# Turning attention weights on VectorE and through DRAM instead of on TensorE, with the order of every engine written out

## The chip, the cores and the metric

One core of one Trainium2 chip runs the kernel. The metric is device time in microseconds (us), the median of the runs on the chip; a profiled execution gives the traces that are quoted.

## The reference

```python
# q, k, v: (8, 8, 576, 64) fp32: batch, heads, sequence, head dimension
scores = q @ k.T / 8
thresh = max(scores, -1) - tau                        # tau = 0.02
scores = where(scores >= thresh, scores, -1e9)
attn = exp(scores - max(scores)); attn /= attn.sum(-1) + 1e-9
x = (attn @ v)  -> (4608, 512)                        # heads side by side
h = x @ w_in                                          # 512 -> 2048
g = where(h > 0, h, exp(min(h, 0)) - 1)
return g @ w_out                                      # 2048 -> 512
```

## The kernel before

Work goes in steps of 128 query rows (the 64 left over rows of two heads share a step, a half step) of a pair of heads: five steps a pair, 20 a sequence, 160 in all. A step computes scores, their maximum, the exponentials, masks them (`w`), normalises, and turns the 128 x 1152 weights on TensorE, so that keys lie on the partitions for the product with `v`. A whole sequence's result then goes through the feed-forward part in 32 units of four 512-column matmuls (in the profile a matmul of fp32 shows as two records). From step 20 the units are mixed in between the attention steps, so that TensorE has work during the waits of attention. The weights w_in and w_out arrive as 64-bit floats and are converted on the way, in the first 35 steps.

```python
    # ... (pools, constants, weight conversion, loads of q, k, v are cut)
    def begin(pr, i, hs):
        qT, kT, qd = pairs[pr][:3]
        if hs[0] == 0:
            open_steps[pr, i] = {
                "w": att.tile([P, 2, 2, HALF], FP32, name="w"),
                **{x: small.tile([P, 2], FP32, name=x) for x in ("mx", "nb", "th", "sm", "rs")},
            }
        st = open_steps[pr, i]
        cs = slice(hs[0], hs[-1] + 1)
        scs = {h: psum["s"].tile([P, 2, 512], FP32, name="sc") for h in hs}
        for a in range(2):
            for h in hs:
                k0 = a * HALF + (0 if h else TAIL)
                r, qs = (slice(h * D, (h + 1) * D), qT[:, i * P : (i + 1) * P]) if i < NC else (slice(0, P), qd)
                nc.tensor.matmul(scs[h][:, a, :HALF], qs[r], kT[r, k0 : k0 + HALF], start=True, stop=True)
        for h in hs:
            nc.vector.tensor_reduce(st["mx"][:, h : h + 1], scs[h][:, :, :HALF], axis=AX.XY, op=ALU.max)
        nc.gpsimd.tensor_scalar(st["nb"][:, cs], st["mx"][:, cs], nkeep, 1.0, ALU.mult, ALU.mult)
        nc.gpsimd.tensor_scalar(st["th"][:, cs], st["mx"][:, cs], 1.0, ntau, ALU.mult, ALU.add)
        for h in hs:
            e = att.tile([P, 2, HALF], FP32, name="e", bufs=3)
            nc.scalar.activation(e, scs[h][:, :, :HALF], AF.Exp, bias=st["nb"][:, h : h + 1], scale=keep)
            st[h] = scs[h], e

    def finish(pr, i, hs):
        st = open_steps[pr, i]
        cs = slice(hs[0], hs[-1] + 1)
        w, sm, rs = st["w"], st["sm"], st["rs"]
        for h in hs:
            sc, e = st.pop(h)
            nc.vector.scalar_tensor_tensor(w[:, h], sc[:, :, :HALF], st["th"][:, h : h + 1], e, ALU.is_ge, ALU.mult,
                                           accum_out=sm[:, h : h + 1])
        nc.vector.tensor_scalar(sm[:, cs], sm[:, cs], 1e-9, None, ALU.add)
        nc.vector.reciprocal(rs[:, cs], sm[:, cs])
        for h in hs:
            nc.gpsimd.tensor_scalar(w[:, h], w[:, h], rs[:, h : h + 1], 1.0, ALU.mult, ALU.mult)

    def transpose(dst, src):
        nc.tensor.matmul(dst, src, ident, is_transpose=True, skip_group_check=True)

    def turn(pr, i):
        w = open_steps.pop((pr, i))["w"].rearrange("p h a n -> p (h a n)")
        if i == 0:
            wTs[pr, 0] = wtp.tile([P, 2 * NC + 1, 2 * P], FP32, name="wTa")
        if i == 2:
            wTs[pr, 1] = wtp.tile([P, 2 * NC + 1, 2 * P + TAIL], FP32, name="wTb")
        wT = wTs[pr, min(i // 2, 1)]
        n0 = i % 2 * P if i < NC else 2 * P
        if i < NC:
            cs = slice(n0, n0 + P)
            for h in range(2):
                rt = ps_t.tile([P, NC, P], FP32, name="rt", tag="rt")
                for c in range(NC):
                    k0 = h * (S + TAIL) + c * P
                    transpose(rt[:, c], w[:, k0 : k0 + P])
                nc.scalar.copy(wT[:, h * NC : (h + 1) * NC, cs], rt)
            rt = ps_t.tile([P, NC, P], FP32, name="rt", tag="rt")
            transpose(rt[:, 0], w[:, MAIN : MAIN + P])
            nc.scalar.copy(wT[:, 2 * NC, cs], rt[:, 0])
        else:
            # ... (second part of the odd tile of 64 + 64 query rows is cut)

    def values(pr, part):
        b, j = divmod(pr, NPAIR)
        vm, vd = pairs[pr][3:]
        wT = wTs.pop((pr, part))
        if b not in xts:
            xts[b] = xpool.tile([P, KJ, MAIN], FP32, name="xt")
        n = wT.shape[2]
        pv = ps_t.tile([P, 512], FP32, name="pv", tag="rt")
        nc.tensor.matmul(pv[:, :n], vd, wT[:, 2 * NC], start=True, stop=False, skip_group_check=True)
        for c in range(NC):
            for h in range(2):
                nc.tensor.matmul(pv[h * D : (h + 1) * D, :n], vm[:, h, c], wT[:, h * NC + c],
                                 start=False, stop=(c == NC - 1), skip_group_check=True)
        nc.scalar.copy(xts[b][:, j, part * 2 * P : (part + 1) * 2 * P], pv[:, : 2 * P])
        if part:
            # ... (tail columns are cut)

    def ffn1(g, ft):
        while progress[1] < (ft // 4 + 1) * KJ:
            convert_w()
        xt = xts[g] if g < B else xtail
        ph = psum["f"].tile([P, 512], FP32, name="ph", tag="f")
        for j in range(KJ):
            nc.tensor.matmul(ph, w_in_sb[:, j, ft * P : (ft + 1) * P], xt[:, j], start=(j == 0), stop=(j == KJ - 1))
        e = epool.tile([P, MAIN], FP32, name="fe")
        nc.scalar.activation(e, ph, AF.Exp)
        nc.vector.tensor_scalar(e, e, 1.0, -1.0, ALU.min, ALU.add)
        gt = gts[ft] = gpool.tile([P, MAIN], FP32, name="gt")
        nc.vector.scalar_tensor_tensor(gt, ph, 0.0, e, ALU.max, ALU.add)

    # ... (first sequence, heads one by one, is cut); then, steps 20 to 161:
    due = 0.0
    rate = (NFT + NIT * NFT // 4) / (per_seq - 1)
    for n in range(per_seq, len(steps) + 2):
        if n < len(steps):
            ahead(*steps[n])
            begin(*steps[n], [0, 1] if steps[n][1] < NC else [0])
            convert_w()
            convert_w()
            finish(*steps[n], [0, 1] if steps[n][1] < NC else [0])
        if n - 1 < len(steps):
            turn(*steps[n - 1])
        behind(*steps[n - 2])
        due = min(due + rate, len(units))
        while due >= 1 and units:
            f, a = units.popleft()
            f(*a)
            due -= 1
```

The scheduler of the language orders the instructions of each engine.

## Time and profile before

| | before |
|---|---|
| median of the runs | 1615.66 us (three runs; 1614.61 with the fourth, used below) |
| span of the profiled run | 1611.8 us |
| TensorE busy | 97% |
| VectorE, ScalarE, GpSimd busy | 46%, 36%, 24% |
| a sequence of 20 steps, once steady | 178.6 us |

How to read the groups: source line, engine, operation, output <- inputs, shapes, number; then busy time in us and mean ns of one; then the idle time of that engine just ahead of them and what ended it. In a timeline the columns are start and length in us, engine, line, operation, tiles and number, and in brackets the idle time before. Matmuls overlap their neighbours, so what one costs is the distance to the next start.

### The profile page before, as it was taken

To read this page: it belongs to the slowest core of one execution; us is meant where nothing else is said; L and a number is where in the kernel's file an instruction comes from. 1 tells how busy PE (TensorE), PEld (TensorE's weight loads), DVE (VectorE), ACT (ScalarE), POOL (GpSimd) and SP (SyncE) were. 2 spreads that over 40 slices of the span, in tenths; PEclk is the share of its full clock that TensorE was granted. 3 is DMA by queue.
4 is the path that set the end of the run, shared out by engine and by line. 5 is a ranking of instruction groups with operands and counts; after the bars stand their busy time and mean duration, and the time that the engine had idled before them with its cause. 6 is when DMAs were issued, how large, how long until landed. Compare 5 with 4: busy or idle time off the path is not lost.

```text
span 1611.8 us, 17586 instructions
## 1 busy us (share of the span) xinstructions
PE 1570.4 (97%) x5952; PEld 786.4 (49%) x5952; DVE 735.0 (46%) x1670; ACT 586.1 (36%) x1109; POOL 379.6 (24%) x779
## 2 busy tenths in 40 slices
PE   7899889999999999999999999999999999999998
PEld 4554444554454445544555544554555454444443
DVE  6778773455335543455335543455345533220210
ACT  4665653343334433344334433344234333110110
POOL 4654552221222212222122212212122222000000
PEclk8999999999999999999999999999999999999999
DMA  5334541111111101110111011111110000000000
GB/s 108 69 81 104 142 130 36 32 19 23 29 29 29 23 15 36 36 23 15 30 35 30 15 25 27 34 23 23 28 34 10 9 7 14 7 1 20 7 7 20
DMA packets 200553, 55.68 MB, mean 35 GB/s; under 512 B 191760, under 2 KB 191760, under 8 KB 200464
## 3 DMA queue, kind: packets, MB, share of 16 engines
q1 hardware_dynamic: 200464, 54.56, 15.2%
q8 instruction: 48, 0.79, 0.2%
q14 instruction: 41, 0.34, 0.1%
HBM read 45.09 MB, written 9.44 MB: 34 GB/s over the span
## 4 chain that ended last, share of the span: by engine, by line
PE 82%; DVE 7%; POOL 4%; ACT 2%; issue 2%; DMA 1%; SPq 1%; POOLq 0%; DVEq 0%; ACTq 0%
PE po L299 30%; PE ph L285 26%; PE sc L197 9%; PE rt L221 8%; PE pv L269 8%; DVE w L213 3%; POOL w L218 2%; PE pv L266 2%; DVE mx L199 1%; ACT e L204 1%; POOL wtop L134 1%; DMA wst<-in_moe_w_out_dram 1%; DVE gt L290 1%; ACT fe L287 1%; DVE fe L288 1%
## 5 line engine op out<-in xcount | busy, mean ns | idle before, releaser
L299 PE MATMUL po<-w_out_sb,gt 128*128 128x512 f32 x1152 | 520.0, 597 | 0.0
L285 PE MATMUL ph<-xt,w_in_sb 128*128 128x512 f32 x1024 | 464.1, 597 | 0.0
L199 DVE TENSOR_REDUCE mx<-sc 128x1 f32<-128x576 f32 x288 | 207.4, 751 | 304.7 <-PE sc L197 304.6
L299 PEld LDWEIGHTS po<-w_out_sb,gt 128*128 128x128 f32 x1152 | 209.7, 191 | 236.5 <-issue 236.0
L218 POOL TENSOR_SCALAR w<-w,rs 128x576 f32<-128x576 f32 x288 | 217.0, 763 | 357.3 <-DVE rs L216 326.8
L213 DVE SCALAR_TENSOR_TENSOR w<-sc,th,e 128x576 f32<-128x576 f32 x288 | 226.5, 815 | 158.5 <-ACT e L204 150.8
L285 PEld LDWEIGHTS ph<-xt,w_in_sb 128*128 128x128 f32 x1024 | 184.7, 190 | 204.0 <-issue 203.0
L204 ACT ACTIVATE e<-sc,nb,keep 128x576 f32<-128x576 f32 x288 | 227.4, 829 | 83.8 <-POOL nb L200 83.5
L221 PE MATMUL rt<-ident,w 128*128 128x128 f32 (+1 forms) x1344 | 211.5, 284 | 17.9 <-POOL w L218 12.0
L221 PEld LDWEIGHTS rt<-ident,w 128*128 128x128 f32 (+1 forms) x1344 | 153.4, 143 | 118.5 <-issue 46.1
L197 PE MATMUL sc<-kT,qT 64*128 64x288 f32 x1024 | 192.9, 439 | 16.6 <-DVE kT L172 8.2
L288 DVE TENSOR_SCALAR fe<-fe 128x512 f32<-128x512 f32 x144 | 63.7, 443 | 315.3 <-ACT fe L287 315.3
L287 ACT ACTIVATE fe<-ph 128x512 f32<-128x512 f32 x144 | 85.9, 596 | 287.8 <-PE ph L285 287.8
L197 PEld LDWEIGHTS sc<-kT,qT 64*128 64x128 f32 x1024 | 107.1, 190 | 127.1 <-issue 84.9
L200 POOL TENSOR_SCALAR nb<-mx,nkeep 128x2 f32<-128x2 f32 (+1 forms) x176 | 52.1, 296 | 480.8 <-DVE mx L199 404.9
L238 ACT COPY wTa<-rt 128x512 f32<-128x512 f32 x128 | 70.9, 587 | 163.1 <-PE rt L221 161.1
L238 ACT COPY wTb<-rt 128x512 f32<-128x512 f32 x128 | 72.2, 584 | 129.3 <-PE rt L221 128.1
L290 DVE SCALAR_TENSOR_TENSOR gt<-ph,fe 128x512 f32<-128x512 f32 x144 | 99.4, 690 | 5.8
L304 ACT COPY ot<-po 128x512 f32<-128x512 f32 x36 | 21.1, 585 | 181.4 <-PE po L299 181.4
L269 PE MATMUL pv<-wTb,vm 128*64 128x320 f32 x512 | 76.0, 439 | 0.0
L269 PE MATMUL pv<-wTa,vm 128*64 128x256 f32 x512 | 63.6, 391 | 0.0
L285 PE MATMUL ph<-xtail,w_in_sb 128*128 128x512 f32 x128 | 55.1, 592 | 0.0
(45 smaller groups left out, 666.7 us busy)
## 6 DMA issues: line engine op xcount, KB each, us to landing
qm<-in_q_dram SPq DMA_DIRECT2D x128, 72.0 KB, 2.6
km<-in_k_dram SPq DMA_DIRECT2D x128, 72.0 KB, 2.5
vm<-in_v_dram SPq DMA_DIRECT2D x64, 128.0 KB, 2.4
wst<-in_moe_w_in_dram SPq DMA_DIRECT2D x16, 512.0 KB, 4.0
wst<-in_moe_w_out_dram SPq DMA_DIRECT2D x16, 512.0 KB, 3.8
out_dram<-ot SPq DMA_DIRECT2D x32, 256.0 KB, 2.0
vd<-in_v_dram SPq DMA_DIRECT2D x64, 16.0 KB, 2.1
out_dram<-ot SPq DMA_DIRECT2D x8, 128.0 KB, 2.3
```

Of the source, the lines that this page charges most:

```text
L197: nc.tensor.matmul(scs[h][:, a, :HALF], qs[r], kT[r, k0 : k0 + HALF], start=True, stop=True)
L199: nc.vector.tensor_reduce(st["mx"][:, h : h + 1], scs[h][:, :, :HALF], axis=AX.XY, op=ALU.max)
L204: nc.scalar.activation(e, scs[h][:, :, :HALF], AF.Exp, bias=st["nb"][:, h : h + 1], scale=keep)
L213: nc.vector.scalar_tensor_tensor(w[:, h], sc[:, :, :HALF], st["th"][:, h : h + 1], e, ALU.is_ge, ALU.mult, accum_out=sm[:, h : h + 1])
L218: nc.gpsimd.tensor_scalar(w[:, h], w[:, h], rs[:, h : h + 1], 1.0, ALU.mult, ALU.mult)
L221: nc.tensor.matmul(dst, src, ident, is_transpose=True, skip_group_check=True)
L238: nc.scalar.copy(wT[:, h * NC : (h + 1) * NC, cs], rt)
L269: nc.tensor.matmul(pv[h * D : (h + 1) * D, :n], vm[:, h, c], wT[:, h * NC + c], start=False, stop=(c == NC - 1), skip_group_check=True)
L285: nc.tensor.matmul(ph, w_in_sb[:, j, ft * P : (ft + 1) * P], xt[:, j], start=(j == 0), stop=(j == KJ - 1))
L287: nc.scalar.activation(e, ph, AF.Exp)
L290: nc.vector.scalar_tensor_tensor(gt, ph, 0.0, e, ALU.max, ALU.add)
L299: nc.tensor.matmul(po[:, :DM], gts[ft][:, it * P : (it + 1) * P], w_out_sb[:, ft], start=(ft == 0), stop=(ft == NFT - 1))
```

## The change

Its intent is to take the transposes off TensorE, the engine that sets the end. From step 35 on VectorE turns the weights in 32x32 squares (`x`), four transfers write the squares to DRAM (`there`) in the order in which the turned tile needs them, and one transfer of the step after reads them back. In place of the scheduler's order stands a written one: step n computes scores, step n-1 turns, step n-2 reads back, step n-3 multiplies with `v`. Two more edits come with it and act from step 20 on: both heads share one score tile with one maximum, and the minimum-and-add of the feed-forward (`fe`) moves from VectorE to GpSimd. The turned tile also gets a new layout from the start, 32 columns to a group, and the conversion of the weights writes into its input's buffer in place of one of its own.

```diff
-            nc.vector.tensor_reduce(st["mx"][:, h : h + 1], scs[h][:, :, :HALF], axis=AX.XY, op=ALU.max)
+        nc.vector.tensor_reduce(st["mx"][:, cs], src[:, :, :, :HALF], axis=AX.XY, op=ALU.max)   # both heads
...
+    def turn_squares(pr, i):
+        w = open_steps.pop((pr, i))["w"]
+        x = late["x"].tile([P, NT, NCH, T], FP32, name="x")
+        def turn_part(c0, src, nc_):
+            nc.vector.transpose(x[:, :, c0 : c0 + nc_], src.rearrange("p (c g n) -> p g c n", c=nc_, n=T))
+        if i < NC:
+            turn_part(0, w[:, :MAIN], NC)
+            turn_part(NC, w[:, MAIN : MAIN + P], 1)
+            turn_part(NC + 1, w[:, MAIN + P :], NC)
...
+        there = turns[pr, i] = dram.tile([NT, T, NT, NCH * T], FP32, name="there")
+        for p in range(NT):
+            nc.sync.dma_start(
+                there[:, :, p].rearrange("c k n -> k c n"), x[p * T : (p + 1) * T].rearrange("k c j n -> k c (j n)")
+            )
...
-        nc.scalar.activation(e, ph, AF.Exp)
-        nc.vector.tensor_scalar(e, e, 1.0, -1.0, ALU.min, ALU.add)
-        nc.vector.scalar_tensor_tensor(gt, ph, 0.0, e, ALU.max, ALU.add)
+        return (
+            lambda: nc.scalar.activation(e, ph, AF.Exp),
+            lambda: nc.gpsimd.tensor_scalar(e, e, 1.0, -1.0, ALU.min, ALU.add),
+            lambda: nc.vector.scalar_tensor_tensor(gt, ph, 0.0, e, ALU.max, ALU.add),
+        )
...
-    for name, bufs in (("s", 2), ("f", 2)):
+    for name, bufs in (("s", 1), ("f", 2)):      # "s" is now one tile of four banks
...
+    with tc.manual_schedule():
+        posts = ()
+        for n in range(SWITCH, len(steps) + 3):  # SWITCH is 35
+            step = (*steps[n], heads_of(steps[n][1])) if n < len(steps) else None
+            due = min(due + rate, len(units))
+            if step:
+                scores(*step)
+            for post in posts[:2]:
+                post()
+            if step:
+                exponentials(*step)
+            for post in posts[2:]:
+                post()
+            if SWITCH < n <= len(steps):
+                turn_squares(*steps[n - 1])
+            if SWITCH + 1 < n <= len(steps) + 1:
+                fetch(*steps[n - 2])
+            posts = ()
+            if due >= 1:
+                posts = ffn_unit()
+                due -= 1
+            if step:
+                masks(*step)
+                # ... q or k of the next pair is prepared here
+            for post in posts:
+                post()
+            posts = ()
+            if step:
+                normalize(*step)
+            if n - 3 >= SWITCH:
+                behind(*steps[n - 3])
+            # ... loads of the pair after the next
+            if due >= 1:
+                posts = ffn_unit()
+                due -= 1
```

## The prediction

> **What bounds the kernel now.** I read the page's engine totals and slices first, then the busy time by stretch, then the groups, and last the timeline of two steps. A step is one 128-row block of queries of one pair of heads; a pair has four full steps and one half step, a sequence four pairs (20 steps), the kernel 160 steps.
>
> ```profile
> PE 1570.4 (97%) x5952; PEld 786.4 (49%) x5952; DVE 735.0 (46%) x1670; ACT 586.1 (36%) x1109; POOL 379.6 (24%) x779
> PE   7899889999999999999999999999999999999998
> DVE  6778773455335543455335543455345533220210
> DMA  5334541111111101110111011111110000000000
> ```
>
> TensorE is full from slice 7 (about 250 us) to the end; VectorE is half idle there and the DMA engines nearly idle. Busy time by stretch says it sharper (columns: stretch, length, then PE, PEld, DVE, ACT, POOL, granted clock, DMA share, GB/s):
>
> ```profile
> 210.00:220.00 10.00, 6.98 (x22) 3.96 (x22) 9.07 (x20) 5.74 (x11) 4.55 (x6) 0.84 0.53 136
> 300.00:400.00 100.00, 99.75 (x400) 50.89 (x399) 51.45 (x115) 39.23 (x75) 21.74 (x50) 1.00 0.13 24
> 600.00:700.00 100.00, 99.92 (x407) 50.46 (x406) 42.72 (x101) 35.58 (x70) 23.20 (x50) 1.00 0.15 32
> ```
>
> So there are three stages: to about 250 us VectorE and its chain decide; to 1387 us (the last value matmul) TensorE does, at 99.8%; then it runs the feed-forward part alone. By the order of instructions the change begins at step 35 (pair 7) of 160. In the timeline the maxima of pair 7 start at 265.8 us, and from then a sequence takes 178.6 us (pairs 12, 16, 20, 24, 28 at 493.7, 672.3, 850.9, 1029.5, 1208.0). The groups concerned:
>
> ```profile
> L221 PE MATMUL rt<-ident,w 128*128 128x128 f32 (+1 forms) x1344 | 211.5, 284 | 17.9 <-POOL w L218 12.0
> L199 DVE TENSOR_REDUCE mx<-sc 128x1 f32<-128x576 f32 x288 | 207.4, 751 | 304.7 <-PE sc L197 304.6
> L213 DVE SCALAR_TENSOR_TENSOR w<-sc,th,e 128x576 f32<-128x576 f32 x288 | 226.5, 815 | 158.5 <-ACT e L204 150.8
> L172 DVE STREAM_TRANSPOSE kT<-km 128x576 f32<-128x576 f32 x32 | 24.6, 769 | 1.1 <-DMA km<-in_k_dram 1.1
> L288 DVE TENSOR_SCALAR fe<-fe 128x512 f32<-128x512 f32 x144 | 63.7, 443 | 315.3 <-ACT fe L287 315.3
> ```
>
> The 211.5 us of transposes look like the prize, but a mean of 284 ns overlaps its neighbours. The timeline of TensorE gives the distance from start to start:
>
> ```profile
> 604.59 1.24 PE L197 MATMUL sc<-kT,qT 64*128 64x288 f32 x8
> 605.76 1.09 PE L221 MATMUL rt<-ident,w 128*128 128x128 f32 x8
> 606.69 1.02 PE L299 MATMUL po<-w_out_sb,gt 128*128 128x512 f32 x2
> 607.55 0.27 PE L221 MATMUL rt<-ident,w 128*128 128x128 f32 x1
> 607.66 0.62 PE L266 MATMUL pv<-wTa,vd 128*128 128x256 f32 x2
> 608.21 1.95 PE L269 MATMUL pv<-wTa,vm 128*64 128x256 f32 x16
> 610.09 2.84 PE L299 MATMUL po<-w_out_sb,gt 128*128 128x512 f32 x6
> ```
>
> Eight transposes take 0.93 us, the ninth 0.11: some 0.116 us each. In the same way: scores 1.17 us (half step 0.97), the value matmuls of the first part 2.43, of the second 2.96, one feed-forward unit (8 records of about 0.43) 3.45.
>
> **What the Trainium skill says.** "TensorE: Matmul & The Clock Gate", Part 4, gives about 275 ns for a transpose in a kernel; the trace agrees on the duration (284), yet what one costs here is the 116 ns pitch. "VectorE: DVE Perf Modes", The three transpose paths: VectorE turns 32x32 blocks only, which is why DRAM must put the squares in place. The trace has the operation at 769 ns for 576 columns. The clock page's Part 1 says an idle window of about 3.4 us halves the TensorE clock: the trace agrees in its first stage (0.84 at 210 us, TensorE 70% busy) and grants 1.00 later; so gaps under 2 us should be harmless. "SBUF — State Buffer", Who interferes with whom: a VectorE instruction with at most one SBUF input outside the two-port modes does not block GpSimd. The squares are such; the removed L288, at 443 ns for 512 elements, runs faster than one element a cycle and may well have been in such a mode. No run shows the lock.
>
> **The change, part by part** (steps 35 to 159: 125 steps, 6.25 sequences).
> 1. Removed: 42 transposes a pair, 168 a sequence, at 0.116 = 19.5 us a sequence; ACT's copies of them (about 1.44 us a step) go too, beside the path. Added on TensorE: one value matmul of 384 in place of 320 columns, 0.2 us a sequence. TensorE's own work becomes 178.6 - 19.3 = 159.3 us a sequence: 122 us over 6.25 sequences is the most there is.
> 2. Added on VectorE: the pitch in this trace is columns / 0.96 plus about 110 ns (mask and sum: 608.68 to 609.42). A full step's squares, 512 + 128 + 512 columns, are then 0.64 + 0.24 + 0.64 = 1.53 us; both heads' maximum in one instruction is 1.31 instead of 1.42. VectorE a step: 1.31 + 1.53 + masks 1.57 + sums 0.37 + up to two gelu-like combinations (gt) at 0.64 + 0.3 for q and k = 6.4 at most, against 8.0 of TensorE: not the bound on average.
> 3. The new ring. The score tile is one buffer of four banks for both heads, so scores of step n+1 wait for the second mask of step n, and in VectorE's written order the previous step's squares stand before that mask. From start of scores: 1.27 (to the maximum) + 1.31 + 1.53 + 1.57 + 0.12 (semaphore) = 5.8 us, 6.4 with a gt between. The exponentials are beside it (maximum + 1.4 us). A step with two feed-forward units keeps TensorE at work for 1.17 + 6.9 = 8.0: no wait. A step with one unit and no value matmuls offers 4.6 and stops for 1.2 (1.8 with gt). I counted the written order: in each 20 steps five are like that (four at 1.2, one at 1.8), **6.6 us a sequence**; two at the start of the new order have no unit at all, and 7 us are lost once.
> 4. q and k preparation now stands ahead of GpSimd's part of the feed-forward: a gt comes about 0.3 us late for its PSUM buffer once a sequence, 0.3 us.
> 5. DRAM. A step writes 576 KB in four transfers and reads them back in one. The trace has 512 KB landing in 4.0 us and 0.36 us to issue one such store. The read issued in step m-1 comes after its squares (4.1 to 4.7) and four issues (1.5), lands 4.4 us later, or 6.5 if it queues behind the writes: 10 to 13 us after step m-1 began. Step m needs it after scores and one unit: at 8.0 + 4.6 = 12.6 after a full step, but at 5.8 + 4.6 = 10.4 after a one-unit step, which precede five of eight value groups. I choose 3 us a sequence (possible: 0 to 10).
> 6. Steps 0 to 34 keep the TensorE transposes; there copies with more pieces and the joint score tile cost, GpSimd's taking L288 gains: I set 0, within 8 us either way.
>
> Sum: 159.3 + 6.6 + 0.3 + 3 = 169.2 us a sequence, 9.4 less than before, times 6.25 = 59 us; less 7 at the start = 52. The base of 178.6 exceeds its own terms (111 units, 22.6 scores, 21.6 values, 19.5 transposes = 175) by 3.5 us of small gaps, some of which the transposes cause, so I take a gain of 60: **1555 us**.
>
> **Rivals.** (a) Everything hides: TensorE stays at 99.8% and the whole 122 us come: about 1495. For it: VectorE's idle half; against it: the ring in 3, whose terms are all measured ones. (b) VectorE becomes the bound: if the strided squares cost twice the plain transpose, the ring is 8.0 and every step is tight: some 12 us a sequence more, about 1610 to 1630. For it: no row has this access pattern; against it: the blocks are still 32 columns in a row. (c) The trip through DRAM takes the transposes' place as a wait: 10 us a sequence, about 1600. For it: 1.18 MB a step, some 140 GB/s where 24 to 32 flow now; against it: the first stage moved 136 GB/s without full engines. (d) Gaps bring the clock down: needs 3 us gaps, seen only at the switch.
>
> **Range and chances.** The terms 3 and 5 have a spread of some 20 us each over the kernel, step 6 of 8: 8 in 10 from 1522 to 1595. Faster than 1583 (2%): 0.80; within 2%: 0.16; slower: 0.04, only by (b) with (c).
>
> **What would show it.** Right: transposes on TensorE 294 instead of 1344; a sequence of 165 to 171 us; TensorE 93 to 96% busy between 300 and 1300 us, its waits on the second mask (VectorE w) of 1 to 2 us, five a sequence; squares of 512 columns at about 0.7 us; granted clock 1.00. Wrong: value matmuls waiting for the tile from DRAM for more than 20 us in all (c); squares over 1.1 us or VectorE over 85% busy (b); no wait at all (a); or the first stage longer by over 10 us.

## The result, and the profile after

The changed kernel takes 1594.14 us in the median of 4 runs (1591.76 to 1595.41), against 1614.61 before. The ratio is 0.9871 (95% interval 0.9844 to 0.9898): ratios here are the mean time of one kernel's runs over that of the other's runs of the same rounds, so not quite the ratio of these medians. Executions over 1.5% slower than the fastest of the same kernel are left out of the means. It is a gain of 20 us, within 2%, where 60 were forecast.

The page of the changed kernel, totals and slices:

```profile
PE 1469.3 (92%) x4902; PEld 678.9 (43%) x4902; DVE 848.9 (53%) x1814; ACT 446.6 (28%) x780; POOL 655.0 (41%) x923
PE   7998888979999999988999899989999999999998
POOL 4666664125621563245423552255225531340430
DMA  5433431375776757676777666766767555000000
```

The 101 us of TensorE's busy time did go, and TensorE is at 92 to 96% where it was at 99.8%. But GpSimd is up from 380 to 655 us, and the first slices of TensorE are no fuller. The groups (the squares are L295, the transposes L247, the joint maximum L220, the moved minimum-and-add L360):

```profile
L360 POOL TENSOR_SCALAR fe<-fe 128x512 f32<-128x512 f32 x144 | 277.3, 1926 | 241.6 <-ACT fe L359 236.7
L295 DVE STREAM_TRANSPOSE x<-w 128x512 f32<-128x512 f32 x250 | 169.5, 686 | 2.8 <-POOL w L244 2.8
L220 DVE TENSOR_REDUCE mx<-sc 128x2 f32<-128x1152 f32 x112 | 151.9, 1356 | 244.3 <-PE sc L210 243.7
L247 PE MATMUL rt<-ident,w 128*128 128x128 f32 (+1 forms) x294 | 53.7, 316 | 16.3 <-POOL w L244 13.4
```

The squares cost what was foreseen (0.69 us for 512 columns), and the transposes are down to 294. One `fe` costs 1.93 us on GpSimd; on VectorE it cost 0.44. Where the time went is read from the start of each step (its first maximum on VectorE) in both traces, in us:

| stretch | before | changed | difference |
|---|---|---|---|
| to step 20 (attention alone) | 109.6 | 112.1 | +2.4 |
| steps 20 to 34 (feed-forward and weight conversion mixed in, old order) | 156.2 | 176.8 | **+20.6** |
| step 35 to the start of the last value matmul (the new order) | 1120.9 | 1074.2 | **-46.7** |
| from there to the end (feed-forward alone) | 225.1 | 228.8 | +3.7 |
| one steady sequence | 178.6 | 170.1 | -8.5 |

The new order brings 47 us, near the 52 that the prediction had for it. The rest was lost before it begins, and a little at the end. The start of the new order was dearer than its steady part: TensorE stood still for 5.2 us at 333 us, for 2.9 us at 341 us, and the granted clock was at half for 13.7 us from 333.3 us on. Every kernel with the new order shows such a start, and part of what lies between 46.7 us and 6.25 x 8.5 = 53 us may come from it; no run separates that. In the new order, TensorE waits as foreseen in kind. Its timeline around two of the waits before scores (a step with one unit and no value matmuls ends in each):

```profile
453.59 3.70 PE L371 MATMUL po<-w_out_sb,gt 128*128 128x512 f32 x8
458.83 1.24 PE L210 MATMUL sc<-kT,qT 64*128 64x288 f32 x8 [1.54 <-DVE w L235]
...
479.62 3.70 PE L371 MATMUL po<-w_out_sb,gt 128*128 128x512 f32 x8
484.93 1.21 PE L210 MATMUL sc<-kT,qd 128*128 128x288 f32 x4 [1.61 <-DVE w L235]
```

I summed such stops over five sequences (distance from one matmul's start to the next, less the usual distance, where over 0.25 us). A sequence has five of them before scores, 1.7 to 1.8 us each, 8.8 in all; 1.4 us before a feed-forward matmul that waits for a buffer in PSUM, the memory that matmuls write to; 1.9 us before value matmuls that wait for the tile from DRAM; 12.1 together. (For the last kind the trace names other instructions as what ended the wait; but in all seven of these stops the tile's transfer had landed 0.1 to 0.25 us before.) 170.1 - 12.1 leaves 158.0 us of TensorE's own work.

The ring itself, in the timeline of all engines in one such step:

```profile
621.30 1.24 PE L210 MATMUL sc<-kT,qT 64*128 64x288 f32 x8
622.59 1.36 DVE L220 TENSOR_REDUCE mx<-sc 128x2 f32<-128x1152 f32 x1 [6.53 <-PE sc L210]
623.86 1.29 DVE L295 STREAM_TRANSPOSE x<-w 128x512 f32<-128x512 f32 x2
624.34 1.55 ACT L225 ACTIVATE e<-sc,nb,keep 128x576 f32<-128x576 f32 x2 [2.35 <-POOL nb L221]
625.08 0.33 DVE L305 STREAM_TRANSPOSE x<-w 128x64 f32<-128x64 f32 x2
626.00 0.82 DVE L235 SCALAR_TENSOR_TENSOR w<-sc,th,e 128x576 f32<-128x576 f32 x1 [0.59 <-ACT e L225]
626.74 0.81 DVE L235 SCALAR_TENSOR_TENSOR w<-sc,th,e 128x576 f32<-128x576 f32 x1
627.71 1.24 PE L210 MATMUL sc<-kT,qT 64*128 64x288 f32 x8 [1.54 <-DVE w L235]
```

From scores to scores are 6.41 us, not the 5.8 of the prediction: the first mask here starts 0.11 us after *both* exponentials are done, and the squares end 0.6 us earlier. In the kernel before it started 0.1 us after the first one. This holds for all 76 full steps from 60 to 154: the first mask never starts sooner than 0.10 us after the second exponential in the changed kernel, and in the kernel before it starts 0.10 us or a little more after the first one. Why the changed kernel waits for both was not tested. So all five stops are alike, with or without a `gt` in between.

Now the stretch that lost 20.6 us. The timeline of the changed kernel in it, cut to one chain:

```profile
200.92 1.92 POOL L360 TENSOR_SCALAR fe<-fe 128x512 f32<-128x512 f32 x1 [1.54 <-ACT fe L359]
...
204.39 1.29 POOL L140 TENSOR_TENSOR wtop<-wtop,wst 128x512 int32<-128x512 int32 x1 [1.56 <-DVE rs L238]
...
205.66 2.00 POOL L244 TENSOR_SCALAR w<-w,rs 128x576 f32<-128x576 f32 x2
...
206.99 1.96 PE L247 MATMUL rt<-ident,w 128*128 128x128 f32 x8 [2.78 <-POOL w L244]
```

Here `fe` holds GpSimd for 1.92 us, `gt` on VectorE follows it, the conversion of the weights comes after that, then the normalisation, and TensorE's transposes stand still for 2.78 us until it is done. So the suspect is the move of `fe` (theory G). Its rivals were the joint score tile (J), which takes effect in the same step 20, and the scheduler's order or the new layout of the turned tile (O).

### The profile page after: what moved, and what is told of

Same layout as the page of the kernel before. It is cut to its first block, busy times and chain, and to the rows that moved or that the text cites. A ratio compares the mean times of both kernels' runs of the same rounds, so it can differ in the third digit from the quotient of the medians.

```text
span 1591.9 us, 16071 instructions
## 1 busy us (share of the span) xinstructions
PE 1469.3 (92%) x4902; PEld 678.9 (43%) x4902; DVE 848.9 (53%) x1814; ACT 446.6 (28%) x780; POOL 655.0 (41%) x923
## 4 chain that ended last, share of the span: by engine, by line
PE 62%; DVE 9%; POOL 4%; DMA 4%; issue 3%; ACT 3%; SPq 2%; DVEq 0%; POOLq 0%; ACTq 0%
PE po L371 26%; PE ph L355 20%; PE sc L210 7%; PE pv L335 7%; DVE w L235 3%; POOL fe L360 3%; DVE mx L220 2%; PE pv L331 2%; ACT e L225 2%; DVE x L295 2%; DMA km<-in_k_dram 2%; SPq L308 1%; DMA qm<-in_q_dram 1%; DMA wTb<-there 1%; ACT fe L359 1%
## 5 line engine op out<-in xcount | busy, mean ns | idle before, releaser
L355 PE MATMUL ph<-xt,w_in_sb 128*128 128x512 f32 x1024 | 470.7, 608 | 11.3 <-DVE gt L361 11.3
L360 POOL TENSOR_SCALAR fe<-fe 128x512 f32<-128x512 f32 x144 | 277.3, 1926 | 241.6 <-ACT fe L359 236.7
L220 DVE TENSOR_REDUCE mx<-sc 128x2 f32<-128x1152 f32 (+1 forms) x176 | 199.8, 1136 | 266.8 <-PE sc L210 266.3
L355 PEld LDWEIGHTS ph<-xt,w_in_sb 128*128 128x128 f32 x1024 | 188.7, 192 | 248.6 <-issue 217.6
L210 PE MATMUL sc<-kT,qT 64*128 64x288 f32 x1024 | 187.5, 448 | 55.0 <-DVE w L235 46.5
L295 DVE STREAM_TRANSPOSE x<-w 128x512 f32<-128x512 f32 (+1 forms) x350 | 182.5, 568 | 2.9 <-POOL w L244 2.8
L247 PE MATMUL rt<-ident,w 128*128 128x128 f32 (+1 forms) x294 | 53.7, 316 | 16.3 <-POOL w L244 13.4
L338 ACT COPY xt<-pv 128x256 f32<-128x256 f32 x64 | 23.8, 372 | 140.7 <-PE pv L335 140.7
L181 POOL COPY qd<-qT 64x64 f32<-64x64 f32 x64 | 15.4, 241 | 108.3 <-DVE qT L177 106.0
L247 PEld LDWEIGHTS rt<-ident,w 128*128 128x128 f32 (+1 forms) x294 | 37.9, 159 | 47.0 <-POOL w L244 23.4
```

Source lines behind the costliest of these rows:

```text
L220: nc.vector.tensor_reduce(st["mx"][:, cs], src[:, :, :, :HALF], axis=AX.XY, op=ALU.max)
L295: nc.vector.transpose(x[:, :, c0 : c0 + nc_], src.rearrange("p (c g n) -> p g c n", c=nc_, n=T))
L360: lambda: nc.gpsimd.tensor_scalar(e, e, 1.0, -1.0, ALU.min, ALU.add),
```

## The experiments

Eight kernels ran. Those of 1 to 4 shared one chip and the runs of the kernel before, those of 5 to 8 another set.

**1. `fe` back on VectorE in steps 0 to 34 only.**

```diff
-            lambda: nc.gpsimd.tensor_scalar(e, e, 1.0, -1.0, ALU.min, ALU.add),
+            lambda: (nc.gpsimd if "x" in late else nc.vector).tensor_scalar(e, e, 1.0, -1.0, ALU.min, ALU.add),
```

> The changed kernel with the minimum-and-add of the feed-forward (fe) put back on VectorE, only in steps 0 to 34 (before the new order starts). In the changed kernel these steps 20 to 34 take 176.8 us against 156.2 before, and one fe takes 1.93 us on GpSimd against 0.44 on VectorE. Theory G (the move of fe to GpSimd, which there also holds the weight conversion's add of 1.29 us and the normalisation, is what the first stage lost): steps 20 to 34 back to 155 to 162 us, total 1572 to 1580. Rival J (the joint score tile and the joint maximum cost the first stage its time): steps 20 to 34 within 5 us of 176.8, total 1589 to 1597. Rival O (the scheduler's order or the new layout of the turned tile): the same as J.

It took 1575.81 us (1571.04 to 1581.12, ratio to before 0.9766). Steps 20 to 34 took 157.1 us. The busy times in that stretch (columns: stretch, length, then busy us of PE, PEld, DVE, ACT, POOL, granted clock, DMA share, GB/s) for the kernel before:

```profile
109.70:265.90 156.20, 141.06 (x528) 70.42 (x528) 110.93 (x227) 81.06 (x148) 71.01 (x94) 0.95 0.42 107
```

for the changed kernel:

```profile
112.00:288.80 176.80, 149.12 (x545) 72.73 (x543) 103.55 (x197) 83.32 (x164) 103.57 (x107) 0.91 0.34 91
```

and for this experiment:

```profile
107.70:264.80 157.10, 138.91 (x545) 67.55 (x544) 107.68 (x214) 83.75 (x164) 73.97 (x91) 0.98 0.40 102
```

Sixteen `fe` fall in the stretch; 16 x (1.93 - 0.44) = 24 us, and GpSimd is busy 30 us less without them. Most of it came out as time, 19.7 us. The clock is part of it: 0.91 with the stops, 0.98 without. This is what theory G expects, and neither J nor O. O was not tested by itself, nor was the shared buffer of the weight conversion: what this run leaves for them is 0.9 us (157.1 against 156.2).

**2. Two score tiles and one maximum a head in steps 20 to 34, as before.**

```diff
-        if "f" in psum:
+        if "x" in late:
             both = psum["s"].tile([P, 2, 2, 512], FP32, name="sc")
...
-    for name, bufs in (("s", 1), ("f", 2)):
-        psum[name] = ctx.enter_context(tc.tile_pool(name=f"ps_{name}", bufs=bufs, space=PSUM))
+    mid = ExitStack()
+    psum["f"] = ctx.enter_context(tc.tile_pool(name="ps_f", bufs=2, space=PSUM))
+    psum["s"] = mid.enter_context(tc.tile_pool(name="ps_s", bufs=2, space=PSUM))
...
+    mid.close()
+    psum["s"] = ctx.enter_context(tc.tile_pool(name="ps_late", bufs=1, space=PSUM))
```

> The changed kernel with two score tiles of two banks and one maximum per head, as in the kernel before, in steps 20 to 34; joint only once the new order starts. Rival J: steps 20 to 34 back to 155 to 162 us, total 1572 to 1580. Theory G and rival O: within 5 us of the changed kernel, 1589 to 1599.

It took 1595.88 us (1588.73 to 1600.39), and steps 20 to 34 took 180.5 us. The joint tile is not the cause there: J falls.

**3. The kernel before with `fe` moved to GpSimd, and nothing else.**

```diff
-        nc.vector.tensor_scalar(e, e, 1.0, -1.0, ALU.min, ALU.add)
+        nc.gpsimd.tensor_scalar(e, e, 1.0, -1.0, ALU.min, ALU.add)
```

> The kernel before with only the fe instruction moved from VectorE to GpSimd, nothing else. Theory G: steps 20 to 34 longer by 15 to 25 us, total 1632 to 1645 (a few us of it at the end, where the feed-forward runs alone). Rivals J and O: within 5 us of 1615.

It took 1683.9 us (1677.93 to 1696.12, ratio 1.0433), so theory G is right in direction and my number was too small. Steps 20 to 34 took 174.0 us (+17.8) and the end 228.9 (+3.8), as expected. Not foreseen was that a steady sequence went from 178.6 to 186.1 us. There TensorE had been at 99.8%; now it stands still four times a sequence: twice, 2.8 us together, for a PSUM buffer that the late `gt` frees, and twice, 3.2 us together, before scores that wait for VectorE's mask. One of each:

```profile
552.71 3.81 POOL L288 TENSOR_SCALAR fe<-fe 128x512 f32<-128x512 f32 x2
554.66 0.69 DVE L290 SCALAR_TENSOR_TENSOR gt<-ph,fe 128x512 f32<-128x512 f32 x1 [3.58 <-POOL fe L288]
555.41 1.12 PE L285 MATMUL ph<-xt,w_in_sb 128*128 128x512 f32 x2 [0.95 <-DVE gt L290]
...
629.38 1.94 PE L197 MATMUL sc<-kT,qT 64*128 64x288 f32 x8 [1.60 <-DVE w L213]
```

The profiled run also lost 17.1 us before step 20, where there is no `fe` at all. In it 48 us of these 127 ran at a half clock, in the kernel before 17 of 110. The timed runs without a profile were 9 to 18 us faster than this one; what brought the clock down there stays open.

**4. The units dealt out by the kind of step: one where value matmuls stand, two elsewhere.**

```diff
-            due = min(due + rate, len(units))
+            due = min(1 if n % NB in (2, 4) else 2, len(units))
```

> The changed kernel with the feed-forward units dealt out by the kind of step in the new order: one in a step with value matmuls, two in any other (8 x 1 + 12 x 2 = 32 a sequence, as many as before). Ring theory (TensorE waits for the second mask only in steps with one unit and no value matmuls): the waits for VectorE's mask before scores, 1.7 to 1.8 us five times a sequence in the changed kernel, disappear; the fe of the preparation steps on GpSimd may cost 1 to 3 us twice a sequence in their place; a sequence of 162 to 166 us instead of 170.4; total 1545 to 1572. Rival (the ring is limited by VectorE's whole load, so the waits only move): 168 to 171 us a sequence, total 1588 to 1598.

It took 1547.7 us (1546.48 to 1555.7, ratio 0.9591), a sequence 162.8 us. The five stops before scores are gone: no stop of over 0.25 us is left there. In their place are two a sequence of 1.5 and 3.0 us after the step that prepares k, 4.5 together, as expected:

```profile
716.78 1.16 PE L210 MATMUL sc<-kT,qd 128*128 128x288 f32 x4
720.82 5.40 PE L355 MATMUL ph<-xt,w_in_sb 128*128 128x512 f32 x8 [2.88 <-DVE gt L361]
```

These eight matmuls take 5.23 us to the next start instead of 3.43. After this stop the clock is at half for 3.4 us, and four of the eight are each some 0.4 us late. The stops for DRAM fell from 1.9 to 0.2 us a sequence as well. So the ring theory holds, and the waits of the new order came from the dealing of the units, not from VectorE's load.

**5. `fe` on VectorE everywhere.**

```diff
-            lambda: nc.gpsimd.tensor_scalar(e, e, 1.0, -1.0, ALU.min, ALU.add),
+            lambda: nc.vector.tensor_scalar(e, e, 1.0, -1.0, ALU.min, ALU.add),
```

> The changed kernel with fe on VectorE everywhere. Theory G says that fe on GpSimd costs something after step 35 too: 1.4 us a sequence for the PSUM buffer of the feed-forward, and 4 us in the feed-forward that runs alone at the end (228.8 against 225.1 us). So against the run with fe on VectorE only early (1576): 8 to 16 us less, 1560 to 1568. If VectorE became too full by it (0.44 us more for each of 16 fe a sequence, in the ring): 1576 to 1590.

It took 1562.81 us (1559.31 to 1565.35, ratio 0.966). Steps 20 to 34 took 157.9 us, a sequence 168.2 (the stop for a PSUM buffer is gone, those before scores are still 8.9 us), the end 225.2. That is 31 us below the changed kernel and next to the 1555 of the prediction.

**6. Edits 4 and 5 together.**

> The changed kernel with both edits that helped: fe on VectorE everywhere and the units dealt out by kind of step. The waits of TensorE named so far then have no cause left: a sequence of 157 to 160 us (the floor of 158 that the gaps leave), steps 20 to 34 at 155 to 162 us, the end at 225 us: total 1494 to 1512. Rival (the ring gets too long with fe in it: 6.4 + 0.44 + 0.44 against 8.0 of TensorE leaves little): a sequence of 161 to 166, total 1515 to 1545.

It took 1490.81 us (1485.24 to 1495.94, ratio to before 0.9221, interval 0.9167 to 0.9276), correct, and so beats both kernels. A steady sequence is 156.7 us in each of five, and no stop of over 0.25 us is left in them. Its totals and slices:

```profile
PE 1441.9 (97%) x4902; PEld 681.0 (46%) x4902; DVE 902.9 (60%) x1958; ACT 448.5 (30%) x780; POOL 387.0 (26%) x779
PE   7998988979999999999999999999999999999998
DVE  6867775457865786578756776678557862210310
```

It came out 3 us under the low end of what I had written. 178.6 - 156.7 = 21.9 us a sequence is the 19.3 of the transposes and 2.6 more; that these are small gaps which went with the transposes is likely, but not shown. VectorE at 60% and the DMA engines at 56% are no hindrance.

**7 and 8. What is slow in `fe` on GpSimd?**

```diff
-            lambda: nc.gpsimd.tensor_scalar(e, e, 1.0, -1.0, ALU.min, ALU.add),
+            lambda: nc.gpsimd.tensor_scalar(e, e, 1.0, -1.0, ALU.mult, ALU.add),    # 7, wrong on purpose
+            lambda: nc.gpsimd.tensor_scalar(e, e, -1.0, 0.0, ALU.add, ALU.min),     # 8
```

> A probe, wrong result on purpose: the changed kernel with fe on GpSimd as multiply-and-add in place of minimum-and-add; same tile, same constants. If the minimum is what GpSimd does slowly: 0.66 to 0.80 us for one fe (the normalisation, multiply and multiply, has 0.76 for 576 columns) and steps 20 to 34 near 160 us. If two constants or the tile make it slow: still 1.9 us.

> The changed kernel with fe on GpSimd as add -1, then minimum with 0: the same values. If a minimum anywhere makes it slow: 1.9 us; if only a minimum as the first operation: 0.66 to 0.80 us.

Each ran once, state unknown: 1561.84 and 1596.25 us. The group of probe 7, multiply and add:

```profile
L360 POOL TENSOR_SCALAR fe<-fe 128x512 f32<-128x512 f32 x144 | 91.0, 632 | 324.8 <-ACT fe L359 321.1 <-DVE wtop L134 1.2 <-POOL kT L188 0.2
```

and of probe 8, add and minimum:

```profile
L360 POOL TENSOR_SCALAR fe<-fe 128x512 f32<-128x512 f32 x144 | 277.5, 1927 | 242.6 <-ACT fe L359 237.8 <-DVE wtop L134 1.2 <-POOL kT L188 0.2
```

The minimum is the slow part, as the first operation or the second; multiply and add on the same tile take a third. With 0.63 us steps 20 to 34 take 161.4 us. The total equals that of experiment 5 by luck of the stretch before step 20, which was 11 us shorter; from step 20 on the probe is 7.5 us behind. So the move to GpSimd would have cost little if GpSimd did a minimum as fast as a product.

The stretches of all runs, in us:

| | to step 20 | steps 20 to 34 | 35 to last values | end | a sequence |
|---|---|---|---|---|---|
| before | 109.6 | 156.2 | 1120.9 | 225.1 | 178.6 |
| changed | 112.1 | 176.8 | 1074.2 | 228.8 | 170.1 |
| 1 | 107.7 | 157.1 | 1075.4 | 229.0 | 169.9 |
| 2 | 116.0 | 180.5 | 1073.3 | 228.9 | 170.2 |
| 3 | 126.7 | 174.0 | 1164.7 | 228.9 | 186.1 |
| 4 | 105.0 | 176.4 | 1034.4 | 228.8 | 162.8 |
| 5 | 116.1 | 157.9 | 1064.4 | 225.2 | 168.2 |
| 6 | 113.0 | 158.1 | 997.2 | 224.9 | 156.7 |
| 7 | 105.0 | 161.4 | 1068.7 | 224.9 | 168.9 |
| 8 | 111.4 | 176.7 | 1077.5 | 228.9 | 170.8 |

The first column varies by some 10 us among kernels that differ little or nothing there. In it the half clock lasted from 0 to 24 us in these runs (not counting run 3), so it should not be read as an effect of an edit.

## Why the prediction was right or wrong

The forecast of 1555 us was wrong by 39 us, at the far end of its range; a gain of 60 us was foreseen and 20 came. By its steps:

- **Step 1** (transposes, 19.5 us a sequence) was right. TensorE's own work was set at 159.3 us a sequence and measured 158.0 in the changed kernel, 156.7 with no stop left. (Its 122 us over 6.25 sequences should read 121.)
- **Step 2** (VectorE) was right: a full set of squares was set at 1.53 us and the timelines show 1.49 to 1.63. Rival (b) is refuted.
- **Step 3** (the ring) was right in its mechanism, in the five places, and in the step without a unit; experiment 4 shows it. Its size was too small: 8.8 us a sequence instead of 6.6, since "The exponentials are beside it" fails: the first mask waits for both. That is 14 us over the kernel. The start of the new order, set at 7 us, showed stops of 8.1 us and 13.7 us at half clock besides.
- **Step 4** set 0.3 us for GpSimd's part in the preparation steps and measured 1.4, because one `fe` takes 1.93 us.
- **Step 5** (DRAM) set 3 us a sequence; 1.9 were measured. Rival (c) is refuted: a transfer back took 4.8 to 5.0 us and mostly hid.
- **Step 6 is the one that failed**: "GpSimd's taking L288 gains: I set 0, within 8 us either way". It cost 20.6 us in steps 20 to 34, and experiments 1 and 5 put it down to that instruction, while 2 clears the joint tile that the same step suspected. The prediction weighed only what VectorE would gain; it set no duration for the instruction on GpSimd, whose other row of the kind, a product, suggested 0.7 us. It then left out that this stage hangs on a chain through GpSimd, not on VectorE's load.
- The sum had nothing for the end of the kernel, where `fe` costs 3.7 us more (experiment 5 brings it back).

The account closes as a sum: the new order gave 46.7 us where 52 net were foreseen (59 less 7), the extra 8 us that I added for gaps did not show, and the first stretches and the end took 26.7 us where 0 was set (2.4 of it, before step 20, within the scatter of that stretch). That is 20.0 of gain. With `fe` on VectorE the same change gains 52 us (experiment 5), near the forecast.

On the clock the prediction took from the Trainium skill ("TensorE: Matmul & The Clock Gate", Part 1: the clock halves after an idle window of about 3.4 us) that gaps under 2 us are harmless, and read the trace before as agreeing. The runs do not bear this out. In the trace before, the clock fell at 216.9 us within a stop of 2.6 us. In the steady part of the changed kernel stops of up to 2.1 us did leave the granted clock at 1.00. But in experiment 2 and in probes 7 and 8 one stop of 1.9 to 2.2 us each was followed by 3.4 us at half clock; in experiment 1 a stop of 2.8 us was not, and in experiment 4 four of six stops of 2.8 to 3.2 us were. So the length of a stop alone does not decide, and what does stays open.

## What to carry to other kernels

Before an instruction moves to another engine, find a row of that very operation on that engine, or measure it; a row of another operation of the same form may be off by a factor of three. A stage that hangs on a chain of engines pays for most of such a move (18 to 20 of 24 us here), while a stage that TensorE fills hides most of it (in experiment 3 it paid 7.5 of 24 us a sequence). And where work is dealt out between steps by an even rate, deal it by what each step lacks instead: in the stretch that it touches that one line was worth 40 us with the slow instruction in place and 67 without it (46 and 72 in the medians of the whole kernel, where the stretch before step 20 scatters).

## What the Trainium skill lacked or had wrong

- "GPSIMD Engine Reference", 4.1 Engine selection, says that elementwise work with one input is "roughly line-rate" on GpSimd. For multiply and add on 128x512 fp32 the runs show 0.63 us. For minimum and add, or add and minimum, they show 1.93 us, against 0.44 on VectorE. The row of that section names add, mul and max, but no minimum.
- "TensorE: Matmul & The Clock Gate", Part 4, has a transpose's duration (about 275 ns, for bf16; here 284 ns in the mean) but not what one costs in a row of them, 116 ns here for fp32.
- The same page, Part 1, has the clock halve after an idle window of about 3.4 us. In probe 7 a stop of 1.92 us was followed by 3.4 us at half clock.
- "VectorE: DVE Perf Modes", The three transpose paths, has a bf16 figure alone. For fp32 in 32x32 squares the runs show 0.69 us for 512 columns with the squares scattered over the output, no dearer than a plain one (0.77 us for 576).
- No page measures a tile's trip to DRAM and back: 144 KB written landed in 2.5 us and 576 KB read back in 4.8 to 5.0 us (medians), with the DMA engines 52% busy over the whole run.
